# Block-sparse attention with routed experts and a feed-forward: scores over the used keys alone, masks and identity loaded once, another order of loads

## The chip, the cores and the metric

The kernel runs on one core of a Trainium2 chip. The metric is the device time of one launch in microseconds (us). The kernel before took 432.42 us as the median of three runs (431.78, 432.42 and 434.9).

## What is computed

Three layers follow one another. Shapes: batch 2, 8 heads, 576 positions, 64 columns per head; so 1,152 tokens of 512 columns.

```python
scores = q @ k.T / 8                              # per batch and head
mask_local   = (0 <= i - j) & (i - j < 32)        # heads 0 to 3
mask_strided = (0 <= i - j) & (i % 32 == j % 32)  # heads 4 to 7
attn = softmax(where(mask, scores, -1e9)) @ v     # heads side by side: x [1152, 512]
e = argmax(x @ w_gate);  gate = max(softmax(x @ w_gate))   # one of 8 experts
y = gate * (relu(x @ w1[e]) @ w2[e])              # w1 [8, 512, 1024], w2 [8, 1024, 512]
h = y @ w_in;  out = (h - tanh(h)) @ w_out        # w_in [512, 2048], w_out [2048, 512]
```

## The kernel before

Attention comes first, then routing, the experts and the feed-forward. The change touches attention alone, and the loads that are issued during it.

**Tiles.** Two heads of a batch are worked on together as a *pair*; there are eight, in the order of line 282: two local ones, four strided ones, two local ones. A local pair has nine tiles: 128 rows (64 positions of two heads) against the 96 keys that they can see. A strided pair has eleven tiles: positions are sorted by their remainder modulo 32, and a tile has 108 rows (three remainders times 18 positions of two heads) against the 54 keys of the same remainders. Tiles are worked on in *groups* of three (local) or four, four and three (strided): 24 groups, numbered 0 to 23, three per pair, so groups 3, 6, 9, 12 and 15 are the first of pairs 1 to 5.

**A group's steps.** `attn_scores` writes the mask of the whole group into a PSUM bank with one bfloat16 matmul by the identity, and then adds each tile's scores with one float32 matmul, which the trace shows as two instructions. The mask and the scores are as wide as a tile has rows: 128 or 108 columns, though only 96 or 54 are read afterwards. VectorE and ScalarE do the softmax. Three groups later `attn_probs_t` transposes the probabilities on TensorE with the float32 identity `identf`; five groups later `attn_values` multiplies them with the values. Seven groups after a pair's last group (`logits_pair`, n - LAG2 - 2) the rows of x are transposed back, multiplied with the gate's weights (both in one matmul against `iw`, which holds identity and gate side by side) and stored to DRAM by SP. The loop at line 523 issues these steps in this order, and each engine's instructions keep it.

**Loads.** All but one are issued by SP in program order; an issue that waits holds up those behind it. Queries and keys have two buffers, values three (`vts`), so a pair's load waits for the scores of the pair before the last. `load_qk` for pair i + 1 is called at the first group of pair i, its values (`load_v`) at the last. The first pair comes in pieces, and between them the masks, of which the loads bring all six local tiles and the strided ones; behind them pair 0's values, the identity in four copies (256 KB) and the gate. SP hands at most eight transfers to the queue before the oldest has landed. The two halves of the first expert's first weights (`load_w`, 1,024 KB each) are issued at groups 6 and 9, at group 9 behind the stores of pair 0's rows of x; from group 10 on their conversion to two float16 parts runs in between on ScalarE and VectorE.

**POOL** clears the unused rows of value and probability buffers at the start and has nothing to do in attention after that.

**Names and lines.** The masks and the identity: lines 111 to 114. Clearing on POOL: lines 243 to 251. `load_qk`: 253 to 271. First loads: 283 to 287. `attn_scores`: 289 to 319. The loop and the calls of `load_w`: 523 to 564. In the trace the instructions of all engines but SP have line 75, that of a helper, so they are told apart by their tiles: `kt,qt` the scores, `mk` the masks, `iw,pr` the transposes, `ptl,vt` and `ptr,vt` the values, `iw,xT` the logits, `st` a half of expert weights, `xd<-xw` the stores of x.

Of the kernel before, what the change touches and what calls it, by code (L numbers as in the profile page):

```python
# [8 lines left out]
BF16 = mybir.dt.bfloat16  # L9
# [12 lines left out]
E, F1 = 8, 1024  # L22
# [36 lines left out]
# h - tanh(h) by odd powers of h from the third on  # L59
# [5 lines left out]
class _Last:  # L65
    """An engine that remembers its last instruction."""
# [15 lines left out]
def kernel(  # L82
# [12 lines left out]
    @contextmanager  # L95
    def behind():
        # what the block adds on ACT and DVE is issued after what they have so far
        with tc.issue_after(act.last.ins), tc.issue_after(dve.last.ins):
            yield
# [11 lines left out]
    iw = cst.tile([P, NCH, P + E], F32, name="iw")  # L111
    identf = iw[:, 0, 0:P]
    mk = cst.tile([P, 3 * P + 3 * P + 4 * SM + P], BF16, name="mk")
    identb, ml0, mlb, msb = mk[:, 0:P], mk[:, P:4 * P], mk[:, 4 * P:7 * P], mk[:, 7 * P:]
# [14 lines left out]
    # sums of the low parts: not finite where a high part is not  # L129
# [4 lines left out]
    # sums of squares of a part of each operand, over their least  # L134
# [25 lines left out]
    def f64_split(hi, lo, raw, scale, n=512):  # L160
        # the bits of -w 2^128 as a float32; sizes from 1 on come out as not finite. A shift by three leaves the two
        # top bits of the exponent set; the last three bits of the fraction are the top ones of the low word
# [34 lines left out]
    def get_w(w, e, n=2):  # L197
        # the halves, and what splits them bit by bit
# [24 lines left out]
    KT = STRIDE + S + 64  # L223
    vts = [pa1.tile([P, NST * P], F32, name=f"vt{i}") for i in range(3)]
# [5 lines left out]
    # the clock of the products' array rises while the first rows are on their way  # L230
# [11 lines left out]
    # rows past the keys stay zero: the products take all 128 rows  # L242
# [6 lines left out]
    pool.memset(vts[2], 0.0)  # L249
    for t in ptr:  # L250
        pool.memset(t, 0.0)

    def load_qk(b, hp, first=False):
        qt = pa.tile([P, NST * P], F32, tag="q", name="qt")
        kt = pa.tile([P, KT], F32, tag="k", name="kt")
        if first:
            # what the first group of tiles takes goes first
            sp.dma_start(mk[:, :4 * P], masks[:, :4 * P])
            sp.dma_start(qt[:, : 3 * P], q_loc[b, hp, :, :3 * P])
            nc.scalar.dma_start(kt[:, :2 * P], k_loc[b, hp, :, :2 * P])  # L260
            sp.dma_start(mk[:, 4 * P:], masks[:, 4 * P:])
            sp.dma_start(kt[:, 2 * P:], k_loc[b, hp, :, 2 * P:])
            for j in (3, 6):
                sp.dma_start(qt[:, j * P:(j + 3) * P], q_loc[b, hp, :, j * P:(j + 3) * P])
        elif hp < 2:
            sp.dma_start(qt[:, : NLT * P], q_loc[b, hp])
            sp.dma_start(kt, k_loc[b, hp])
        else:
            sp.dma_start(qt[:, : NST * SM], q_str[b, hp - 2])
            sp.dma_start(kt[:, : NST * SN], k_str[b, hp - 2])  # L270
        return qt, kt
# [9 lines left out]
    # the last ones are local: only their last tiles' tokens wait for the end  # L281
    pairs = [(0, 0), (0, 1), (0, 2), (0, 3), (1, 2), (1, 3), (1, 0), (1, 1)]
    qks = {0: load_qk(*pairs[0], first=True)}
    vs_ = {}
    vs_[0] = load_v(0, *pairs[0])
    sp.dma_start(iw[:, :, 0:P], ident_d)
    sp.dma_start(iw[:, :, P:P + E], w_gate)

    def attn_scores(b, hp, tiles, qt, kt):
# [3 lines left out]
        w = nq  # L293
        sc = bank()
        mask = msb if not loc else (ml0 if tiles[0] == 0 else mlb)
        pe.matmul(sc[:, : n * w], identb, mask[:, : n * w], start=True, stop=False, skip_group_check=True)
        for j, i in enumerate(tiles):
            k0 = 64 * i if loc else SN * i
            wk = min(w, NST * SN - k0) if not loc else w
# [757 lines left out]
```

## Time and profile before

| | |
|---|---|
| median of three runs | 432.42 us (431.78 to 434.9) |
| profiled execution, its span from the first to the last instruction | 432.6 us (no other time of this execution is given) |
| TensorE (PE) matmuls busy | 399.6 us, 92% |
| VectorE (DVE) busy | 298.4 us, 69% |
| ScalarE (ACT) busy | 261.6 us, 60% |
| GpSimd (POOL) busy | 39.3 us, 9% |
| moved by DMA | 69.92 MB, mean 162 GB/s |
| granted TensorE clock, mean | 0.969 of 2.4 GHz |

Attention is about the first 82 us, routing and the first gather reach to 104 us, the experts to 240 us, the feed-forward to the end. Busy shares over the whole span say little here, because attention, a fifth of the span, has other limits than the rest. The page's row of granted clock shows three dips, in the slices around 15, 45 to 50, and 100 us. Sizes in the views of transfers are in units of 1,024 bytes; GB/s are of 10^9 bytes. A matmul's own duration includes its way through the array, so the spacing of a stream is read from the start of one to the start of the next.

### The profile page before, as it was taken

Reading aid. Unit: us, or ns where it says so; the run is one execution under the profiler, and the core shown is the slowest. Engines: PE = TensorE matmul, PEld = TensorE weight load, DVE = VectorE, ACT = ScalarE, POOL = GpSimd, SP = SyncE. Lnnn points to the kernel's source line nnn. Section 1 sums busy time; section 2 is a strip of 40 time slices with the busy share of each in tenths; the row PEclk is TensorE's granted clock in tenths of the full one; section 3 lists DMA queues with packets and bytes.
Section 4 is the critical chain, followed back from the end, with each engine's and each line's share of the span. In section 5 each row is a group of like instructions: output and inputs, shape, how many; then the busy total and the mean of one; then the engine's idle time right before and its main releaser. Section 6 shows DMA issues by size and latency. Waiting matters only on the chain.

```text
span 432.6 us, 8410 instructions
## 1 busy us (share of the span) xinstructions
PE 399.6 (92%) x3192; PEld 298.5 (69%) x3192; DVE 298.4 (69%) x752; ACT 261.6 (60%) x612; POOL 39.3 (9%) x44
## 2 busy tenths in 40 slices
PE   6699598864999999999999999999999999999994
PEld 3598598723999999999999566665444655444441
DVE  2388589772898979899999799999983678000000
ACT  3377387443996777876974799899752887100000
POOL 6000000066102011000000000000000100000000
PEclk9699699995999999999999999999999999999998
DMA  8797488626879788789724423312350100000000
GB/s 217 218 295 230 152 269 236 213 93 205 291 262 354 279 291 302 243 302 341 259 101 148 147 97 113 131 59 89 99 194 17 58 1 2 24 27 27 24 26 27
DMA packets 33514, 69.92 MB, mean 162 GB/s; under 512 B 3108, under 2 KB 9252, under 8 KB 33468
## 3 DMA queue, kind: packets, MB, share of 16 engines
q1 hardware_dynamic: 31580, 63.68, 44.7%
q0 software_dynamic: 1744, 5.51, 3.8%
q8 instruction: 27, 0.44, 0.4%
q14 instruction: 19, 0.16, 0.1%
q10 hardware_dynamic: 144, 0.13, 0.1%
HBM read 64.59 MB, written 4.72 MB: 160 GB/s over the span
## 4 chain that ended last, share of the span: by engine, by line
PE 42%; DVE 9%; issue 8%; DMA 3%; ACT 2%; POOL 0%; POOLq 0%; DVEq 0%; ACTq 0%
PE bank L75 42%; DVE w2l L75 3%; DMA xg<-xd,ids 2%; DVE w1l L75 2%; DVE fa L75 2%; DVE hl L75 1%; ACT w2h L75 1%; DMA out_dram<-ob,ids 1%; ACT win_h L75 1%; DVE x2l L75 0%; DVE xl L75 0%; DVE win_l L75 0%; ACT x2h L75 0%; POOL xg L75 0%; POOL out_dram L75 0%
## 5 line engine op out<-in xcount | busy, mean ns | idle before, releaser
L75 PE MATMUL bank<-xh,w1h 128*128 128x192 f16 x256 | 64.0, 250 | 7.6 <-ACT xh L75 7.6
L75 PE MATMUL bank<-xh,w1l 128*128 128x192 f16 x256 | 64.1, 250 | 0.7 <-DVE w1l L75 0.5
L75 PE MATMUL bank<-xl,w1h 128*128 128x192 f16 x256 | 64.0, 250 | 0.0
L75 PE MATMUL bank<-x2l,win_h 128*128 128x384 f16 x192 | 62.6, 326 | 0.5 <-DVE ok L75 0.5
L75 PE MATMUL bank<-hl,w2h 128*128 128x192 f16 x256 | 63.0, 246 | 0.0
L75 PE MATMUL bank<-hh,w2h 128*128 128x192 f16 x256 | 63.0, 246 | 0.0
L75 PE MATMUL bank<-hh,w2l 128*128 128x192 f16 x256 | 63.0, 246 | 0.0
L75 PE MATMUL bank<-x2h,win_h 128*128 128x384 f16 x192 | 62.6, 326 | 0.0
L75 PE MATMUL bank<-x2h,win_l 128*128 128x384 f16 x192 | 62.6, 326 | 0.0
L75 PEld LDWEIGHTS <-win_h 128*128 128x128 f16 x384 | 37.6, 98 | 25.8 <-DVE ok L75 0.7
L75 PE MATMUL bank<-wo_h,gh 128*128 128x512 f16 x144 | 54.6, 379 | 0.0
L75 PE MATMUL bank<-wo_l,gh 128*128 128x512 f16 x144 | 54.6, 379 | 0.0
L75 PE MATMUL bank<-wo_h,gl 128*128 128x512 f16 x144 | 54.6, 379 | 0.0
L75 PEld LDWEIGHTS <-gh 128*128 128x128 f16 x288 | 28.1, 98 | 33.6
L75 PEld LDWEIGHTS <-w1h 128*128 128x128 f16 x512 | 47.2, 100 | 0.3
L75 PEld LDWEIGHTS <-w2h 128*128 128x128 f16 x512 | 46.1, 98 | 0.0
L75 DVE SCALAR_TENSOR_TENSOR fa<-raw,fa 128x512 uint32<-128x512 uint32 x64 | 42.8, 684 | 2.1 <-ACT fa L75 1.7
L75 ACT ACTIVATE ob<-bank 128x512 f32<-128x512 f32 x9 | 5.4, 597 | 62.6 <-PE bank L75 60.1
L75 DVE SCALAR_TENSOR_TENSOR w2l<-st,w2h 128x1024 f16<-128x1024 f32 x32 | 38.8, 1217 | 2.9 <-ACT w2h L75 2.6
L75 DVE SCALAR_TENSOR_TENSOR w1l<-st,w1h 128x1024 f16<-128x1024 f32 (+1 forms) x40 | 38.4, 1003 | 0.3 <-ACT w1h L75 0.2
L75 DVE SCALAR_TENSOR_TENSOR w<-z,y 128x384 f32<-128x384 f32 x48 | 26.0, 552 | 15.2 <-ACT z L75 15.2
L75 PE MATMUL bank<-kt,qt 128*108 128x108 f32 (+2 forms) x160 | 23.5, 292 | 12.1 <-DMA kt<-in_k_str_dram 5.7
(144 smaller groups left out, 765.5 us busy)
## 6 DMA issues: line engine op xcount, KB each, us to landing
st<-in_w_dram SPq DMA_DIRECT2D x32, 1024.0 KB, 5.8
raw<-in_w_in_dram SPq DMA_DIRECT2D x16, 512.0 KB, 5.6
raw<-in_w_out_dram SPq DMA_DIRECT2D x16, 512.0 KB, 3.5
qt<-in_q_str_dram SPq DMA_DIRECT2D x4, 594.0 KB, 6.0
xd<-xw SPq DMA_DIRECT2D x15, 128.0 KB, 2.0
vt<-in_v_loc_dram SPq DMA_DIRECT2D x4, 432.0 KB, 6.1
qt<-in_q_loc_dram SPq DMA_DIRECT2D x3, 576.0 KB, 9.0
kt<-in_k_str_dram SPq DMA_DIRECT2D x4, 297.0 KB, 6.7
```

The costliest lines, as they stand in the source:

```text
L75: self.last = f(*a, **k)
```

## The change

- **Scores.** The score matmuls take the 96 or 54 keys that are read, and the bank is as narrow. The group's mask is read from one tile of the mask, repeated by the access pattern; only the first local group of a pair has its own mask columns.
- **Masks and identity.** Of the masks the first 128 KB are loaded as before, and of the strided one a single tile of 54 columns. The four float32 copies of the identity are no longer loaded, but written by POOL from the bfloat16 one; the gate is loaded to a tile of its own and copied by POOL to its place beside them.
- **Keys.** Keys have two fixed buffers whose margins POOL clears once; loads bring 576 columns and no margins (672 and 594 before).
- **Order on SP.** The first pair's pieces come without masks in between. Pair 1's queries and keys are issued right behind, in front of pair 0's values; its queries come in two pieces with the keys between them. The strided mask, the values and the gate follow.
- **Order on POOL.** The margins first; the three copies after the clearing of `vts[0]`, `vts[1]` and `ptl`; the clearing of `vts[2]` and `ptr` behind the copies.
- **Weights.** The two halves are issued at groups 5 and 8 instead of 6 and 9, that is behind the values of pairs 2 and 3 and in front of the queries and keys of pairs 3 and 4; the second half is now in front of the stores of pair 0's rows of x.

```diff
-    mk = cst.tile([P, 3 * P + 3 * P + 4 * SM + P], BF16, name="mk")
-    identb, ml0, mlb, msb = mk[:, 0:P], mk[:, P:4 * P], mk[:, 4 * P:7 * P], mk[:, 7 * P:]
+    mk = cst.tile([P, 4 * P + SN], BF16, name="mk")
+    identb, ml0, ml1, ms1 = mk[:, 0:P], mk[:, P:4 * P], mk[:, 2 * P:2 * P + KW], mk[:, 4 * P:]
...
+    kts = [pa1.tile([P, KT], F32, name=f"kt{i}") for i in range(2)]
...
+    for t in kts:
+        pool.memset(t[:, :STRIDE], 0.0)
+        pool.memset(t[:, STRIDE + S:], 0.0)
...
-    pool.memset(vts[2], 0.0)
-    for t in ptr:
-        pool.memset(t, 0.0)
-    def load_qk(b, hp, first=False):
+    def load_qk(n, b, hp):
         qt = pa.tile([P, NST * P], F32, tag="q", name="qt")
-        kt = pa.tile([P, KT], F32, tag="k", name="kt")
-        if first:
+        kt = kts[n % 2]
+        def keys(eng, c0, c1):
+            eng.dma_start(kt[:, STRIDE + c0:STRIDE + c1],
+                          k_loc[b, hp, :, STRIDE + c0:STRIDE + c1] if hp < 2 else k_str[b, hp - 2, :, c0:c1])
+        def queries(c0, c1):
+            sp.dma_start(qt[:, c0:c1], (q_loc[b, hp] if hp < 2 else q_str[b, hp - 2])[:, c0:c1])
+        if n == 0:
             sp.dma_start(mk[:, :4 * P], masks[:, :4 * P])
-            sp.dma_start(qt[:, : 3 * P], q_loc[b, hp, :, :3 * P])
-            nc.scalar.dma_start(kt[:, :2 * P], k_loc[b, hp, :, :2 * P])
-            sp.dma_start(mk[:, 4 * P:], masks[:, 4 * P:])
-            sp.dma_start(kt[:, 2 * P:], k_loc[b, hp, :, 2 * P:])
-            for j in (3, 6):
-                sp.dma_start(qt[:, j * P:(j + 3) * P], q_loc[b, hp, :, j * P:(j + 3) * P])
-        elif hp < 2:
-            sp.dma_start(qt[:, : NLT * P], q_loc[b, hp])
-            sp.dma_start(kt, k_loc[b, hp])
+            queries(0, 3 * P)
+            keys(nc.scalar, 0, 2 * P)
+            queries(3 * P, 6 * P)
+            keys(sp, 2 * P, S)
+            queries(6 * P, 9 * P)
+        elif n == 1:
+            queries(0, 3 * P)
+            keys(sp, 0, S)
+            queries(3 * P, 9 * P)
         else:
-            sp.dma_start(qt[:, : NST * SM], q_str[b, hp - 2])
-            sp.dma_start(kt[:, : NST * SN], k_str[b, hp - 2])
+            queries(0, NLT * P if hp < 2 else NST * SM)
+            keys(sp, 0, S)
         return qt, kt
...
-    qks = {0: load_qk(*pairs[0], first=True)}
+    qks = {i: load_qk(i, *pairs[i]) for i in range(2)}
+    wg = cst.tile([P, NCH, E], F32, name="wg")
+    sp.dma_start(mk[:, 4 * P:], masks[:, 7 * P:7 * P + SN])
     vs_ = {}
     vs_[0] = load_v(0, *pairs[0])
-    sp.dma_start(iw[:, :, 0:P], ident_d)
-    sp.dma_start(iw[:, :, P:P + E], w_gate)
+    sp.dma_start(wg, w_gate)
+    pool.tensor_copy(identf, identb)
+    pool.tensor_copy(iw[:, 1:, 0:P], identb.unsqueeze(1).to_broadcast([P, NCH - 1, P]))
+    pool.tensor_copy(iw[:, :, P:], wg)
+    pool.memset(vts[2], 0.0)
+    for t in ptr:
+        pool.memset(t, 0.0)
...
         nq, nk = (P, KW) if loc else (SM, SN)
-        w = nq
         sc = bank()
-        mask = msb if not loc else (ml0 if tiles[0] == 0 else mlb)
-        pe.matmul(sc[:, : n * w], identb, mask[:, : n * w], start=True, stop=False, skip_group_check=True)
+        scv = sc[:, : n * nk].rearrange("p (t k) -> p t k", k=nk)
+        if loc and tiles[0] == 0:
+            mask = ml0.rearrange("p (t k) -> p t k", k=P)[:, :, :nk]
+        else:
+            mask = (ml1 if loc else ms1).unsqueeze(1).to_broadcast([P, n, nk])
+        pe.matmul(scv, identb, mask, start=True, stop=False, skip_group_check=True)
         for j, i in enumerate(tiles):
-            k0 = 64 * i if loc else SN * i
-            wk = min(w, NST * SN - k0) if not loc else w
-            pe.matmul(sc[:nq, j * w:j * w + wk], qt[:, i * nq:(i + 1) * nq], kt[:, k0:k0 + wk],
+            k0 = 64 * i if loc else STRIDE + SN * i
+            pe.matmul(sc[:nq, j * nk:(j + 1) * nk], qt[:, i * nq:(i + 1) * nq], kt[:, k0:k0 + nk],
                       start=False, stop=True, skip_group_check=True)
...
-            if g == 0 and i + 1 < len(pairs):
-                qks[i + 1] = load_qk(*pairs[i + 1])
+            if g == 0 and 1 < i + 1 < len(pairs):
+                qks[i + 1] = load_qk(i + 1, *pairs[i + 1])
...
-        if n in (6, 9):
-            w10.append(load_w(1, n // 9, 0))
+        if n in (5, 8):
+            w10.append(load_w(1, n // 8, 0))
```

## Rows read from the trace of the kernel before

**Rows 1.** Busy time by stretch: engines, granted clock, DMA share, GB/s.

```profile
60.00:80.00 20.00, 18.03 (x157) 16.77 (x156) 18.23 (x85) 14.40 (x63) 0.00 (x0) 1.00 0.89 294
110.00:240.00 130.00, 128.99 (x1561) 127.85 (x1558) 118.85 (x221) 98.61 (x155) 8.80 (x10) 1.00 0.76 261
```

**Rows 2.** Waits of TensorE to 60 us: us in total, times, longest.

```profile
PE bank L75 <- DMA kt<-in_k_str_dram: 5.7, 1, 5.7
PE bank L75 <- DMA kt<-in_k_loc_dram: 5.5, 1, 5.5
PE bank L75 <- DVE zz L75: 1.2, 1, 1.2
```

**Rows 3.** Timeline of TensorE: start, us, instructions, idle before and releaser.

```profile
15.11 1.62 PE L75 MATMUL bank<-kt,qt 128*128 128x128 f32 x6 [5.49 <-DMA kt<-in_k_loc_dram]
...
21.77 0.35 PE L75 MATMUL bank<-mk 128*128 128x432 bf16 x1
...
27.30 0.35 PE L75 MATMUL bank<-mk 128*128 128x432 bf16 x1
27.48 0.92 PE L75 MATMUL bank<-kt,qt 128*108 128x108 f32 x8
...
34.54 0.35 PE L75 MATMUL bank<-mk 128*128 128x432 bf16 x1
...
38.16 0.36 PE L75 MATMUL bank<-mk 128*128 128x432 bf16 x1
...
41.99 0.35 PE L75 MATMUL bank<-mk 128*128 128x432 bf16 x1
47.99 1.75 PE L75 MATMUL bank<-kt,qt 128*108 128x108 f32 x8 [5.66 <-DMA kt<-in_k_str_dram]
...
53.03 0.36 PE L75 MATMUL bank<-mk 128*128 128x432 bf16 x1
```

**Rows 4.** Busy time by stretch, around the second wait.

```profile
42.00:44.00 2.00, 0.34 (x3) 0.00 (x0) 1.45 (x7) 2.00 (x10) 0.00 (x0) 1.00 1.01 320
44.00:46.00 2.00, 0.00 (x0) 0.00 (x0) 1.94 (x7) 1.29 (x5) 0.00 (x0) 0.60 0.98 322
46.00:48.00 2.00, 0.01 (x1) 0.04 (x1) 1.31 (x6) 0.00 (x0) 0.00 (x0) 0.50 0.84 227
50.00:52.00 2.00, 2.00 (x15) 1.99 (x14) 0.33 (x2) 1.45 (x6) 0.00 (x0) 0.69 0.07 29
```

**Rows 5.** Timeline of SP: when transfers are issued.

```profile
0.74 0.39 SPq L258 DMA_DIRECT2D mk<-in_masks_dram  x1
...
21.36 0.41 SPq L270 DMA_DIRECT2D kt<-in_k_str_dram  x1
...
26.89 0.41 SPq L270 DMA_DIRECT2D kt<-in_k_str_dram  x1
32.99 0.39 SPq L391 DMA_DIRECT2D xd<-xw  x1
...
34.66 0.46 SPq L184 DMA_DIRECT2D st<-in_w_dram  x1
...
36.14 0.56 SPq L270 DMA_DIRECT2D kt<-in_k_str_dram  x1
```

**Rows 6.** The same issues (0.74, 21.36, 26.89, 34.66): KB, us to landing.

```profile
mk<-in_masks_dram SPq DMA_DIRECT2D x1, 128.0 KB, 2.7
kt<-in_k_str_dram SPq DMA_DIRECT2D x1, 297.0 KB, 4.2
kt<-in_k_str_dram SPq DMA_DIRECT2D x1, 297.0 KB, 6.7
st<-in_w_dram SPq DMA_DIRECT2D x1, 1024.0 KB, 7.9
```

**Rows 7.** Groups of instructions: busy us, mean ns | idle before; 83 to 85 us.

```profile
L75 PE MATMUL bank<-iw,xT 128*128 128x8 f32 x4 | 0.6, 262 | 0.0
```

**Rows 8.** Timeline of POOL.

```profile
5.33 1.28 POOL L75 MEMSET vt<- 128x1408 f32 x1
```

More of the change, by code (lines that the diff above doesn't have):

```diff
@@ L292, in attn_scores @@
         nq, nk = (P, KW) if loc else (SM, SN)
-        w = nq
         sc = bank()
-        mask = msb if not loc else (ml0 if tiles[0] == 0 else mlb)
-        pe.matmul(sc[:, : n * w], identb, mask[:, : n * w], start=True, stop=False, skip_group_check=True)
+        scv = sc[:, : n * nk].rearrange("p (t k) -> p t k", k=nk)
[4 more added lines that the diff above has]
+        pe.matmul(scv, identb, mask, start=True, stop=False, skip_group_check=True)
         for j, i in enumerate(tiles):
-            k0 = 64 * i if loc else SN * i
-            wk = min(w, NST * SN - k0) if not loc else w
-            pe.matmul(sc[:nq, j * w:j * w + wk], qt[:, i * nq:(i + 1) * nq], kt[:, k0:k0 + wk],
+            k0 = 64 * i if loc else STRIDE + SN * i
+            pe.matmul(sc[:nq, j * nk:(j + 1) * nk], qt[:, i * nq:(i + 1) * nq], kt[:, k0:k0 + nk],
                       start=False, stop=True, skip_group_check=True)
-        scv = sc[:nq, : n * w].rearrange("p (t k) -> p t k", k=w)[:, :, :nk]
+        scv = scv[:nq]
         mx = pa.tile([P, 4], F32, tag="mx", name="mx", bufs=4)
```

## The prediction

> **What bounds the kernel now.** I read the table of stretches first. From 110 to 240 us TensorE is busy 128.99 of 130 us at the full clock [rows 1], so whatever brings the end of attention forward arrives at the end of the kernel nearly undiminished, and a gain must be looked for before that. The waits of TensorE up to 60 us are almost all two waits for keys, 5.5 and 5.7 us [rows 2]. The timeline of TensorE dates them: pair 1's keys let group 3 begin at 15.11, pair 5's let group 15 begin at 47.99, though its mask product stood ready at 41.99 [rows 3]. While TensorE waits, its granted clock falls: 1.00 in 42 to 44 us, 0.60, then 0.50 (the level of 1.2 GHz, down from 2.4), and in 50 to 52 it is still 0.69 [rows 4]. So a wait is paid twice. The keys are late because of what SP issues ahead of them: in front of pair 5's keys (36.14) stand three stores of x that could only be issued from 32.99 on, and the 1,024 KB half of the first expert's weights (34.66) [rows 5].
>
> How fast does the queue deliver? The first mask slice lands at 0.74 + 2.7 = 3.44 us [rows 5, 6]. Pair 1's keys land at 15.11; by the tiles' shapes 2,732 KB stand between the two, which makes 234 KB per us. Later, from pair 3's keys (21.36 + 4.2 = 25.6) to pair 4's (26.89 + 6.7 = 33.6), weights, values, queries and keys are 1,024 + 297 + 594 + 297 = 2,212 KB in 8.0 us: 276 KB per us. The second weight half took 7.9 us from issue to landing, 130 KB per us [rows 5, 6], but it started behind the stores on a queue that had run dry. I take 234 up to pair 2 and the mean, 255, after it; 130 and 276 are kept as ends.
>
> **The change, part by part.**
>
> *Fewer and reordered bytes at the start.* Ahead of pair 1's keys go away: 204 KB of masks, 432 KB of pair 0's values, 256 KB of identity, 16 KB of gate, 384 KB of pair 1's later queries and 96 KB of margins, 1,388 KB. What is left is 1,344 KB, so these keys land at 3.44 + 1344/234 = 9.2 us, not 15.11. Pair 0's values now come behind 2,174 KB, at 12.7. Their first use is at the end of group 5; groups 3 to 5 took 21.77 - 15.11 = 6.7 us at half clock [rows 3], so no less than 3.3 now, 12.5 or later. A few tenths may be lost, and the next wait hides them.
>
> *Where the wait goes.* Pair 2's keys have 3,504 KB in front and land at 18.4. TensorE asks for them between 12.5 and 15.9 (9.2 + 6.7), so it waits 2.5 to 6 us at group 6. That group began at 21.77 [rows 3]: 3.4 us are won so far, not 5.9.
>
> *Weights in front.* Each half now goes ahead of a pair's queries and keys. Small tables (121 KB) end at 18.9. Then values 297, weights 1,024, queries 594, keys 288, that is 2,203 KB: pair 3's keys at 18.9 + 8.6 = 27.5, where group 9 began at 27.30 [rows 3]; TensorE gets there at 18.4 + 5.1 = 23.5 (27.30 - 21.77, less 0.4 for narrower products; at half clock 18.4 + 6.7 = 25.1, which this wait hides). The same bundle again, with the second half in it: pair 4's keys at 36.1, against 34.54 before, TensorE ready at 27.5 + 6.8 = 34.3. Then the stores (288 KB), values, queries, keys, 1,467 KB: pair 5's keys at 41.9. Group 15's turn is 36.1 + 7.1 = 43.2 (41.99 - 34.54, less 0.35), so there is no wait. The second weight half no longer stands behind the stores on SP, and the stores, late anyway, go behind it. Its splits follow from group 16 on and wait for nothing.
>
> So group 15's scores begin at 43.3 in place of 47.99, and without the low clock the way to the next mask is that of group 12, 38.16 - 34.54 = 3.6, less 0.1, not 53.03 - 47.99 = 5.0 [rows 3]. Group 16 stands at 46.8: 6.2 us earlier.
>
> *Narrower scores.* For the mask product the columns are the cost: 432 take 27.48 - 27.30 = 0.18 us, so half of them saves 0.09 per strided group, a quarter of 384 saves 0.04 per local one [rows 3]. For the scores the rows say otherwise. Eight float32 matmuls of 108 moving columns under 108 stationary ones run in 0.92 us, 95 ns apart, and four with only 8 moving columns, but 128 stationary, in 0.6 us at 262 ns each, (0.6 - 0.26)/3 = 113 ns apart [rows 3, 7]. The load of the stationary side sets the pace, and that is not narrowed; I grant only the last matmul of a group, 0.045 and 0.027 us. From group 16 on this is 2 x 0.13 + 6 x 0.067 = 0.6 us; before that it shortens steps that then wait for keys.
>
> The Trainium skill, page TensorE: Matmul & The Clock Gate, section Back-to-back issue gap, has the spacing of an isolated stream go with the moving columns. By it each score matmul would get cheaper by a half (strided) or a quarter (local), which is rival D below; the row with 8 columns speaks against it, and the same page's section on LDWEIGHTS, where the time goes with the stationary columns, agrees with that row.
>
> *Identity on POOL.* Three copies of 128, 384 and 32 columns are not in the trace. A memset of 1,408 columns takes 1.28 us [rows 8]; at that rate they are 0.5 us, at four times that 2.0. The memsets that stay in front of them end at 5.33 now, a few tenths later with the margins', and the first transpose stands behind group 3's scores, after 9.2 us: hidden. The gate's copy waits for the gate's landing (2,190 KB, 12.8 us), and behind it on POOL stands the clearing of the third value buffer, 1.3 us; the load of pair 2's values, and SP's queue behind it with the weights, is released at 14.2. The queue has work until 18.9, so this is hidden with 4 us to spare. Keys in two fixed buffers wait as the rotating ones did; the four margin memsets run in the first 2 us.
>
> *VectorE.* From 60 to 80 us it is busy 18.23 of 20 us [rows 1], and in the second wait it worked off 1.45 + 1.94 + 1.31 = 4.7 us [rows 4]. That respite is gone. I charge 1 us (between 0 and 4.7), near the low end, since before 60 us TensorE never waits for it for longer than 1.2 us [rows 2].
>
> **Sum.** 6.2 + 0.6 - 1 = 5.8 us off. The profiled span is 432.6 us, 0.2 above the median of the three runs, 432.42; so 426.7 us is forecast. With 276 KB per us throughout the later part pair 4's keys come at 34.9 and the gain is 7; with 234 they come at 37.7 and it is 4.2: 425.4 to 428.3.
>
> **Rivals.**
> A, slower: the weights hold the keys up. If each half takes 7.9 us, as the second one did, and the rest goes at 234, a bundle takes 13.0 us: pair 3's keys at 31.9, pair 4's at 44.9, group 16 at 55.5, 2.5 late, with up to 3 more for the clock after a wait of several us: 435 to 438. It decides from about 6.7 us per half. For it: the one landing that the profile shows. Against: the other half lay inside the 8.0 us bundle.
> B, larger gain: the queue delivers what the DMA moved in 42 to 46 us, 320 GB/s [rows 4], 312 KB per us. Then pair 2's keys land at 14.7, pair 3's at 22.2, group 16 comes near 40, 13 us early, and VectorE gives some back: 421. Against: such rates are means over all DMA engines, and a tile is there when the slowest is done.
> C, given back: VectorE needs the 4.7 us that the wait gave it, and the end of attention moves by 2 only: 430.2.
> D, the pace of the score matmuls goes with the moving columns after all: groups 15 to 23 hold 22 strided ones, 0.045 us each, and 36 local ones, 0.027 each, 2.0 us more: 424.7. That is what the first of the two sections of the Trainium skill's page named above would give.
>
> **How the numbers follow.** Forecast 0.52, A 0.13, B 0.13, C 0.17, D 0.05. About 1%, 4.3 us, is what a measurement here can tell from no change. Faster by more than that: B, D and five sixths of the forecast, 0.62. Slower: half of A, 0.06. The rest, 0.32, is within. The range goes from B's 421 to 431.5, past C; it leaves out A and a part of B.
>
> **What would show it.** Right: the first wait for keys gone from 10 to 15 us; waits at groups 6 and 9, ending near 18.4 and 27.5; none at group 15; score matmuls still 95 and about 112 ns apart; group 16's mask near 46.8; the stretch after attention as long as before. Wrong: weight halves landing over 6.7 us after the transfer ahead of them; TensorE waiting for VectorE before group 20; a first transpose that waits for POOL.

## The result and the profile after

The changed kernel takes 428.7 us (median of 20 runs, 424.4 to 432.9), the kernel before in the same session 432.8 (20 runs): ratio 0.9897, 95% interval 0.987 to 0.9924. That is 4.1 us faster, where 5.8 us and 426.7 were forecast: inside the range, 2.0 us above the forecast and 1.5 below rival C (430.2). The steps came out rather differently than forecast.

Profiled span: 426.8 us, of an execution that took 428.67. The table gives the start of the named matmul (or of VectorE's write of the slots' ids) in each trace, in us.

| kernel | median us | ratio to before [95%] | group 16 | last logits | ids | first expert matmul | first of feed-forward | span |
|---|---|---|---|---|---|---|---|---|
| before | 432.78 | | 53.03 | 83.36 | 88.23 | 103.66 | 239.36 | 432.64 |
| after | 428.70 | 0.9897 [0.987, 0.9924] | 42.71 | 75.84 | 80.71 | 96.86 | 233.51 | 426.80 |
| e1_weights_late | 428.47 | 0.9952 [0.992, 0.9984] | 47.60 | 78.18 | 83.05 | 98.07 | 232.66 | 425.93 |
| e2_values_first | 427.79 | 0.9912 [0.9874, 0.9951] | 44.29 | 75.82 | 80.69 | 96.30 | 233.02 | 426.31 |
| e3_wide_scores | 426.53 | 0.9887 [0.9844, 0.993] | 44.77 | 76.66 | 81.53 | 96.81 | 232.11 | 425.38 |
| e5_no_low_parts | 421.03 | 0.9767 [0.9732, 0.9802] | 47.81 | 77.08 | 81.95 | 92.33 | 227.23 | 420.51 |
| e8_bytes_alone | 428.62 | 0.9902 [0.9866, 0.9938] | 50.41 | 80.13 | 85.02 | 100.66 | 236.90 | 430.18 |
| g1_bytes_back | 432.07 | 0.9988 [0.995, 1.0026] | 46.81 | 79.95 | 84.83 | 100.42 | 236.52 | 429.96 |
| e4_early_splits | 421.23 | 0.9727 [0.9686, 0.9769] | 44.37 | 74.74 | 79.61 | 90.36 | 225.99 | 419.64 |
| e7_first_tokens_first | 428.22 | 0.9903 [0.9868, 0.9937] | 42.14 | 75.22 | 80.09 | 87.79 | 231.38 | 424.87 |
| e9_gather_alone | 430.39 | 0.9957 [0.9927, 0.9987] | 42.55 | 75.93 | 80.81 | 88.62 | 232.94 | 426.21 |
| f2_low_parts_later | 422.03 | 0.9758 [0.9721, 0.9796] | 45.05 | 76.63 | 81.51 | 89.98 | 227.94 | 421.23 |
| f3_weights_behind_rows | 425.71 | 0.9852 [0.9815, 0.9889] | 42.81 | 75.74 | 80.62 | 91.96 | 228.89 | 422.18 |
| f4_early_and_later | 420.89 | 0.9757 [0.9709, 0.9806] | 43.58 | 73.98 | 78.85 | 89.34 | 223.39 | 416.68 |

Sessions ran beside different medians of before (432.78; 431.03 for e1, e2, e3, e5; 432.37 for e4, e7, e8, e9; 432.87 for f2 to f4; 432.22 for g1), so kernels are compared by their ratios. One row of a trace is one execution, and those of a kernel differ by up to 8.5 us. Up to the last logits after, e7, e9, f2 and f3 are the same program, and in these five traces group 16 lies at 42.1 to 45.1 and the last logits at 75.2 to 76.6: smaller differences than that between two rows say little. Ratios leave out executions over 1.5% above the fastest of their kernel; one of those left out, of f3, took 1,045 us, which nothing here explains.

The waits of TensorE to 60 us, which answer to [rows 2] (total, times, longest):

```profile
PE bank L75 <- DMA kt<-in_k_str_dram: 3.4, 2, 2.5
PE bank L75 <- DVE nm L75: 2.1, 1, 2.1
PE bank L75 <- DVE zz L75: 1.2, 1, 1.2
```

The two long waits for keys, 11.2 us, have become two short ones of 3.4, and a new one for VectorE has come. The timeline of TensorE, for [rows 3]:

```profile
8.27 0.88 PE L75 MATMUL bank<-kt,qt 128*128 128x96 f32 x6
...
11.23 0.50 PE L75 MATMUL bank<-iw,pr 128*96 128x128 f32 x3 [2.08 <-DVE nm L75]
...
14.42 0.26 PE L75 MATMUL bank<-mk 128*128 128x216 bf16 x1
15.56 0.93 PE L75 MATMUL bank<-kt,qt 128*108 128x54 f32 x8 [0.88 <-DMA kt<-in_k_str_dram]
...
20.75 0.26 PE L75 MATMUL bank<-mk 128*128 128x216 bf16 x1
23.54 1.01 PE L75 MATMUL bank<-kt,qt 128*108 128x54 f32 x8 [2.54 <-DMA kt<-in_k_str_dram]
...
28.41 0.27 PE L75 MATMUL bank<-mk 128*128 128x216 bf16 x1
28.52 0.88 PE L75 MATMUL bank<-kt,qt 128*108 128x54 f32 x8
...
32.08 0.26 PE L75 MATMUL bank<-mk 128*128 128x216 bf16 x1
...
39.22 0.26 PE L75 MATMUL bank<-mk 128*128 128x216 bf16 x1
...
42.71 0.27 PE L75 MATMUL bank<-mk 128*128 128x216 bf16 x1
```

Group 3's scores start at 8.27 without a wait (15.11 before), group 6's at 15.56, group 9's at 23.54; groups 12 and 15 wait for nothing, and group 16 stands at 42.71, 10.3 us earlier. When SP issues, for [rows 5], and the last two issues' time to landing, for [rows 6]:

```profile
8.71 0.43 SPq L261 DMA_DIRECT2D kt<-in_k_str_dram  x1
...
12.16 0.39 SPq L185 DMA_DIRECT2D st<-in_w_dram  x1
...
14.62 0.33 SPq L261 DMA_DIRECT2D kt<-in_k_str_dram  x1
...
19.67 0.38 SPq L185 DMA_DIRECT2D st<-in_w_dram  x1
...
20.64 1.11 SPq L261 DMA_DIRECT2D kt<-in_k_str_dram  x1
...
31.50 0.42 SPq L261 DMA_DIRECT2D kt<-in_k_str_dram  x1
```

```profile
kt<-in_k_str_dram SPq DMA_DIRECT2D x1, 288.0 KB, 10.2
kt<-in_k_str_dram SPq DMA_DIRECT2D x1, 288.0 KB, 5.6
```

Pair 4's keys are there at 20.64 + 10.2 = 30.8 and pair 5's at 31.50 + 5.6 = 37.1, each before its group's turn. The stretches, for [rows 1] and [rows 4] (busy us of PE, PEld, DVE, ACT, POOL; granted clock; DMA share; GB/s):

```profile
42.00:44.00 2.00, 2.00 (x20) 1.68 (x19) 1.91 (x10) 0.35 (x1) 0.00 (x0) 1.00 0.91 338
44.00:46.00 2.00, 2.00 (x22) 2.00 (x22) 1.97 (x10) 1.61 (x9) 0.00 (x0) 1.00 0.05 15
60.00:80.00 20.00, 17.25 (x118) 13.71 (x118) 15.16 (x77) 10.53 (x39) 0.00 (x0) 0.91 0.70 218
100.00:230.00 130.00, 128.68 (x1544) 127.60 (x1542) 115.44 (x216) 97.75 (x153) 8.99 (x10) 0.99 0.77 264
```

Where before TensorE stood still for most of 42 to 46 us, it is busy throughout, at the full clock. From 100 to 230 us it is bound by itself as before.

### The profile page after: what moved, and what is told of

It is laid out like the page before. It is cut to its first block, busy times and chain, and to the rows that moved or that the text cites. A ratio compares the mean times of both kernels' runs of the same rounds, so it can differ in the third digit from the quotient of the medians.

```text
span 426.8 us, 8424 instructions
## 1 busy us (share of the span) xinstructions
PE 398.3 (93%) x3192; PEld 296.9 (70%) x3192; DVE 299.1 (70%) x752; ACT 261.0 (61%) x612; POOL 40.6 (10%) x51
## 4 chain that ended last, share of the span: by engine, by line
PE 61%; DVE 17%; issue 9%; DMA 9%; ACT 3%; POOL 0%; POOLq 0%; DVEq 0%; ACTq 0%
PE bank L75 61%; DMA xg<-xd,ids 4%; DVE w1l L75 3%; DVE w2l L75 3%; DMA kt<-in_k_str_dram 2%; DVE fa L75 2%; DMA qt<-in_q_str_dram 1%; DVE xT L75 1%; DVE hl L75 1%; DVE pr L75 1%; ACT w2h L75 1%; DVE mx L75 1%; DMA out_dram<-ob,ids 1%; ACT win_h L75 1%; DVE rs L75 1%
## 5 line engine op out<-in xcount | busy, mean ns | idle before, releaser
L75 ACT ACTIVATE w2h<-st 128x1024 f16<-128x1024 f32 (+1 forms) x33 | 34.3, 1045 | 0.0
```

The costliest lines, as they stand in the source:

```text
L75: self.last = f(*a, **k)
```

## The experiments

The time has three places: the start (to group 16), the rest of attention (to the last logits), and the way from the ids to the first expert matmul. On that way GpSimd issues *gathers*: transfers that fetch from DRAM the rows of x of an expert's tokens, by the ids, the first two for expert 0, the third and fourth for expert 1. ScalarE scales the rows by their gates, TensorE transposes them, and ScalarE and VectorE write them as two float16 parts, the *columns* that the experts' products take. Expert weights are split the same way: ScalarE writes the *high part*, VectorE the *low part*, in one instruction of about 0.7 us, here called a *split*. The first five kernels take the change apart; the others follow what happened to its gain.

**Weights late again.**
```
-        if n in (5, 8):
-            w10.append(load_w(1, n // 8, 0))
+        if n in (6, 9):
+            w10.append(load_w(1, n // 9, 0))
```


> The changed kernel with the two weight halves issued at groups 6 and 9 again. If bytes and order at the start made the gain and the weights' place is neutral, pair 3's keys no longer wait behind a half (no wait at group 9, 2.5 us in the changed kernel), group 15 waits up to 2 us, group 16 stands at 41 to 43 us (42.71 in the changed kernel) and the time is 428 to 430 us. If the weights' place is what removed the wait at group 15, that wait is back with 4 us or more, group 16 stands at 47 or later, and the time is 431 or more.


The wait for pair 5's keys at group 15 is back, though shorter than the 4 us that were named, and a stretch of low clock with it (1.2 GHz from 39.4 to 46.2 us): the earlier weights are what removed this wait.

```profile
42.25 1.66 PE L75 MATMUL bank<-kt,qt 128*108 128x54 f32 x8 [3.18 <-DMA kt<-in_k_str_dram]
```

Group 16 is 4.9 us later than in the changed kernel, and the last logits only 2.3 us. The ratio is 0.55% above that of the change, and the two intervals overlap by a hair: the earlier weights bring something like 2 us, not shown with certainty.

**Values first.**
```
-    qks = {i: load_qk(i, *pairs[i]) for i in range(2)}
+    qks = {0: load_qk(0, *pairs[0])}
...
     sp.dma_start(wg, w_gate)
+    qks[1] = load_qk(1, *pairs[1])
```


> The changed kernel with pair 1's queries and keys behind the strided mask, pair 0's values and the gate, as the order was before; everything else as changed. If the order of the first loads matters, group 3 waits some 2 us for keys (462 KB more in front, at 234 to 290 KB per us) and group 16 comes 1.5 to 2 us later, time 430 to 431. If softmax sets the start anyway (group 3's transposes waited for VectorE until 11.23), the later keys cost nothing: group 16 within 0.7 us of 42.71 and time 428 to 429.5.


No difference in time (0.9912 against 0.9897). In its trace group 3 does wait for its keys, 2.2 us, and group 16 comes 1.6 us later. The last logits come when those of the changed kernel do (75.82 against 75.84), but only because its last groups of attention ran at the full clock and the changed kernel's did not (below). Pair 1's keys ahead of pair 0's values are worth nothing that can be seen in the time.

**Wide scores.**
```
-        scv = sc[:, : n * nk].rearrange("p (t k) -> p t k", k=nk)
+        w = nq
+        scv = sc[:, : n * w].rearrange("p (t k) -> p t k", k=w)[:, :, :nk]
...
-            pe.matmul(sc[:nq, j * nk:(j + 1) * nk], qt[:, i * nq:(i + 1) * nq], kt[:, k0:k0 + nk],
+            wk = min(w, KT - k0)
+            pe.matmul(sc[:nq, j * w:j * w + wk], qt[:, i * nq:(i + 1) * nq], kt[:, k0:k0 + wk],
```


> The changed kernel with score matmuls 128 and 108 columns wide again (masks stay narrow; the columns past the keys are written and not read). If the load of the stationary side sets their pace, a group gets at most 0.045 us longer, spacing stays 95 and 112 ns, group 16 within 0.5 us of 42.71, time 428.5 to 429.3. If the moving columns set it in the changed kernel, the changed kernel's spacing is 51 and 84 ns and the wide one's groups are 0.36 (strided) and 0.16 (local) us longer, group 16 and the end 1.5 to 2.5 us later.


Ratio 0.9887 against 0.9897: the narrower scores bring nothing measurable. Group 16 was expected within 0.5 us of 42.71 and stands at 44.77; pair 2's keys came at 18.14 there instead of 15.56, with the same bytes in front of them, so the transfers are what differed. Its trace has a strided group of eight score matmuls in 0.92 us, the changed kernel's in 0.88:

```profile
44.88 0.92 PE L75 MATMUL bank<-kt,qt 128*108 128x108 f32 x8
```

**The bytes alone** (the smaller masks, the identity made on GpSimd, the gate's tile, the fixed key buffers; everything else as before): the three edits above together, with pair 1's queries loaded whole.
```
-    qks = {i: load_qk(i, *pairs[i]) for i in range(2)}
+    qks = {0: load_qk(0, *pairs[0])}
...
+    qks[1] = load_qk(1, *pairs[1])
...
-            queries(0, 3 * P)
-            keys(sp, 0, S)
-            queries(3 * P, 9 * P)
+            queries(0, 9 * P)
+            keys(sp, 0, S)
```


> Only one part of the change is kept: the masks' smaller copies, the identity made on GpSimd from the masks' tile, the gate's own tile and the fixed key buffers; the score matmuls are as wide as before, pair 1's queries and keys go behind pair 0's values and the gate, and the weight halves are issued at groups 6 and 9 as before. Theory Q (the queue delivers about 290 KB per us once it is full, and the fewer bytes are most of the gain): pair 1's keys, behind 2,300 KB instead of 2,732, land near 12 to 13 instead of 15.1, pair 2's near 16 to 18, the last wait for keys, at group 15, stays since weights and stores still stand in front of pair 5's keys, and the time is 1 to 2 us below the kernel before. Rival R (the order is what counts): the time is within 0.5 us of the kernel before. Rival V (any order does, since VectorE's work sets the end): the last logits start at 76 to 78 and the time is within 1.5 us of the changed kernel.


Ratio 0.9902, as fast as the changed kernel: 4.2 us of gain, 2.7 to 5.8 by the interval, where theory Q said 1 to 2. The places came as Q had them: pair 1's keys are there at 12.95 (15.11 before), and both long waits for keys remain, 4.6 us at group 3 and 4.9 at group 15. So, as far as one trace goes, removing these waits is not what the time hung on. It is the trace of the longest of this kernel's eight executions, 432.03 us, and its milestones are late for that reason among others. Weights late, which has the fewer bytes too and its weights in the same place, came out at 0.9952; the two intervals overlap, and the runs don't divide the gain more finely than that.

```profile
PE bank L75 <- DMA kt<-in_k_loc_dram: 5.0, 2, 4.6
```

```profile
44.54 1.75 PE L75 MATMUL bank<-kt,qt 128*108 128x108 f32 x8 [4.88 <-DMA kt<-in_k_str_dram]
```

**The bytes back** (orders and narrow scores stay, tables are loaded as before).
```
-            queries(3 * P, 6 * P)
+            sp.dma_start(mk[:, 4 * P:], masks[:, 4 * P:])
+            queries(3 * P, 6 * P)
...
-    sp.dma_start(wg, w_gate)
-    pool.tensor_copy(identf, identb)
...
+    sp.dma_start(iw[:, :, 0:P], ident_d)
+    sp.dma_start(iw[:, :, P:], w_gate)
```


> The changed kernel with its tables loaded as before: all 1,328 columns of the masks ahead of the second part of pair 0's keys, identity and gate by the queue behind pair 0's values, no copies on GpSimd. The orders of keys, values and weights and the narrow scores stay. About 209 KB more stand in front of pair 1's keys and 450 KB in front of pair 2's, 0.7 and 1.6 us at the 290 KB per us seen in the changed kernel. Theory Q (the fewer bytes are the gain, the orders add nothing, as the kernel with the bytes alone was as fast as the changed one): the gain is lost, 431.5 to 432.5 us beside about 432.5 for the kernel before. Rival S (either part is enough, since behind group 16 VectorE's work and then the gathers of rows set the pace and take back whatever comes earlier): the last logits start at 76 to 77.5 and the time stays at 428 to 429.5, ratio 0.988 to 0.993.


Ratio 0.9988: the gain is gone, as theory Q had it, and rival S is out. Group 15 waits no longer, group 16 stands at 46.81, and yet nothing is won by the end. TensorE now waits for the identity in front of its first transposes, since in the new order it stands behind pair 1's keys:

```profile
PE bank L75 <- DMA iw<-in_ident_dram: 4.3, 1, 4.3
```

So the fewer bytes are enough for the gain, and the orders without them bring none in this arrangement; one with the identity in front of pair 1's keys was not run.

**No low parts** (VectorE's low parts of expert 0's first weights are left out, GpSimd fills zeros in their place).
```
-                split_w(w10[i // 4], i % 4, 1)
+                st, hi, lo, sc = w10[i // 4]
+                act.activation(hi[:, i % 4, :], st[:, i % 4, :], AF.Copy, scale=sc)
+                pool.memset(lo[:, i % 4, :], 0.0)
```


> The changed kernel without the low parts of the first expert's first weights: VectorE's eight instructions (0.69 and 0.08 us each, 6.1 us in all, between groups 10 and 20) are left out, POOL writes zeros there, so the output is not the reference's. If VectorE is what gives back the gain of 10 us at group 16 (7.5 left at the last logits), TensorE does not wait for it at groups 21 to 26, the last logits come at 72 to 74 us instead of 75.84, and the time is 424.5 to 427. If something else gives it back, the last logits stay within 0.7 us of 75.84 and the time within 1 us of 428.7.


Ratio 0.9767, 1.3% (5.6 us) below that of the changed kernel, but not where it was looked for: the last logits are no earlier. The fills ran from 8.71 to 12.49, right behind the clearing that began at 6.30, and a tiny instruction of VectorE was held until their end, 5.88 us for what takes 0.17 elsewhere:

```profile
8.71 3.78 POOL L75 MEMSET w1l<- 128x512 f16 x8
```

```profile
6.63 5.88 DVE L75 TENSOR_SCALAR nm<-mx 128x3 f32<-128x3 f32 x1
```

From group 16 to the last logits it is the shortest of all, 29.3 us. Most of its gain came between ids and first expert matmul: 10.4 us instead of 16.1. This opened the second question.

**Early splits.**
```
-    W1_AT = [10, 11, 13, 14, 16, 17, 19, 20]
+    W1_AT = [8, 8, 9, 9, 10, 11, 12, 14]
...
-            if n in W1_AT:
-                i = W1_AT.index(n)
+            for i in [i for i, at in enumerate(W1_AT) if at == n]:
```


> The first weights of expert 0 are split at groups 8 to 14 instead of 10 to 20, into the time up to 32 us in which VectorE was busy 7 to 8 of 10 us; nothing else changes. Theory V (between groups 16 and 26 the work of VectorE, 9.3 to 9.6 of 10 us, sets when the last logits can start; that is where 2.5 of the changed kernel's 10.3 us went): about four splits of 0.69 + 0.08 us leave that stretch, the last logits start at 73 to 74 instead of 75.8 and the time is 2 to 3 us below that of the changed kernel, 424 to 426. Rival T (the chain of each group, scores to values, sets the pace by TensorE itself and its low clock at 68.6 to 72 us): the last logits stay at 75 to 76 and the time within 1 us. Rival W (the splits wait for the second weight half, landed at 28.7, and hold ScalarE and VectorE up): group 12 or 15 comes 1 to 3 us later and the time is 1 to 2 us longer.


421.2 us, ratio 0.9727, the fastest by the ratio and below both kernels. Theory and third rival both hold in part: group 16 is 1.7 us later (no more than one program's traces differ by), the way from there to the last logits 2.8 us shorter (30.4; about 1.5 of that is the low clock, see below), 1.1 us net. The larger part, 5.4 us, lies again behind the ids, where its third gather of rows was not held up.

**First tokens first.**
```
-            act.activation(xg, xg, AF.Copy, scale=gsl[:, a:a + 1])
+            with tc.issue_after(xh_done[0]) if e == 1 else nullcontext():
+                act.activation(xg, xg, AF.Copy, scale=gsl[:, a:a + 1])
...
+        xh_done.append(act.last.ins)
```


> One dependency is added to the changed kernel: on ScalarE the scaling of expert 1's first gathered rows goes behind expert 0's second half of token columns. Theory O (what was won by the end of attention is partly lost again because ScalarE stands 8.04 us in front of that scaling, whose gather of rows lands at 95.69, while expert 0's columns are ready to be made at 87.7): the first expert matmul starts at 88.5 to 90 instead of 96.86, and since the next expert then waits for the same rows, at 97 to 98, some of it is lost again: the time is 3 to 7 us below the changed kernel's, 421 to 425. Rival P (weights or the low parts, not the columns, are the last to be ready): the first expert matmul stays after 95 and the time within 1 us.


The first expert matmul starts at 87.79, 9 us earlier, and the time does not move (0.9903). The wait has only moved: expert 1's transposes stand on TensorE behind the first quarter of expert 0's products, and there it waits 5.9 us for the same rows. A wait was removed, its cause was not.

**Gather alone** (the edit above, and the six splits of expert 1's weights placed behind the first four gathers).


> The kernel with the one dependency on ScalarE, and also the six splits of expert 1's first weight halves put behind the first four gathers of rows. Theory G (GpSimd's third issue of an indirect transfer takes 4.38 us instead of 0.92 because VectorE splits weights at the same time, 84.23 to 88.4 us, and its rows then land behind the weights that the first gather releases): that issue takes about 0.9 to 1.4 us, the rows land near 88 to 90 instead of 95.69, expert 1 finds its columns ready, and the time is 2 to 5 us below that of the kernel with the dependency alone. Rival N (the issue is slow for another reason): it still takes about 4 us and the rows land after 94, the time within 1 us of that kernel, or longer by up to 3 us as the splits come later.


The issue took 0.92 us as expected, the time did not follow (0.9957): ScalarE now had the eight high parts, and pieces of expert 0's second weights, in front of expert 1's rows, and TensorE met the same wait:

```profile
96.88 1.54 PE L75 MATMUL bank<-iw,xg 96*128 96x96 f32 x8 [5.60 <-ACT xg L75]
```

**Low parts later** (only VectorE's six low parts go behind the gathers; ScalarE's high parts stay).
```
-            split_w(w11[i // 4], i % 4, 1)
+            split_hi(w11[i // 4], i % 4)
...
+    with behind():
+        for i in range(NB):
+            split_lo(w11[i // 4], i % 4)
     w1s[1], w2s[0] = [ld[1:3] for ld in w11], [ld[1:3] for ld in w20]
```


> The changed kernel with VectorE's six low parts of expert 1's first weights moved behind the first four gathers of rows; ScalarE's high parts stay where they were. Theory G (VectorE's run of splits holds up the gather that GpSimd issues within a microsecond of its start: in the traces so far that issue ended 0.79 us after the last split, and the weights that the splits release then travel in front of the rows): the third issue takes about 0.9 us instead of 4.4, its rows land near 88 instead of 95.7, the first expert matmul starts at 89 to 91 instead of 96.9, and the time is 4 to 6 us below the changed kernel's, 422 to 425. Attention is untouched, the last logits stay at 75 to 76.5. Rival X (the weights ahead of the rows on the queues alone, not the issue): the issue is short but the rows still land after 93. Rival Y (the low parts, later now, are missed by expert 1): the gain in front of expert 0 is lost again before expert 1 and the time is within 1.5 us.


Theory G's numbers came true: issue 0.92 us, rows at 88.3, first expert matmul at 89.98, 422.0 us (only the last logits, 76.63, are a little later than it said). First the changed kernel's third gather and VectorE's first and last split, then this kernel's (the transfer rows give us to landing):

```profile
84.38 4.38 POOL L75 DMA_INDIRECT xg<-xd,ids  x1 [0.30 <-DVE gsl L75]
```

```profile
84.23 0.68 DVE L75 SCALAR_TENSOR_TENSOR w1l<-st,w1h 128x512 f16<-128x512 f32 x1
...
87.29 0.68 DVE L75 SCALAR_TENSOR_TENSOR w1l<-st,w1h 128x512 f16<-128x512 f32 x1
```

```profile
xg<-xd,ids POOLq DMA_INDIRECT x1, 11.3
```

```profile
85.19 0.92 POOL L75 DMA_INDIRECT xg<-xd,ids  x1 [0.30 <-DVE gsl L75]
```

```profile
xg<-xd,ids POOLq DMA_INDIRECT x1, 3.1
```

In the changed kernel the issue ended at 88.76, 0.79 us after the last split. Its rows came 11.3 us after the issue began, 3.1 without the splits.

**Weights behind rows.**
```
     rows = gather(0)
-    first_gather.append(pool.last.ins)
...
     rows = gather(1)
+    first_gather.append(pool.last.ins)
```


> The changed kernel, with the loads that wait for the first expert's rows made to wait for the second expert's rows as well; the order of every engine stays. Theory G says that both the slow third issue and the weights in front of its rows make them late: with the weights held back the rows land at about 89 + 2.5 = 91.5 instead of 95.7, the first expert matmul starts near 92.7 instead of 96.9, and the time is 2 to 4 us below the changed kernel's, if the held weights (landing some 5 us later) are not missed. Rival I (the slow issue alone, its descriptors being late): the rows still land after 94 and the time is within 1 us or up to 2 us longer.


The issue is as slow as in the changed kernel (4.38 us), the rows land at 90.8 instead of 95.7 and the first expert matmul starts at 91.96: of the 7.4 us that the rows came late (95.7 against 88.3 with the low parts later), about 5 were the weights in front of them. The ratio, 0.9852, is 0.45% below that of the change; the intervals overlap.

**Early and later** (early splits, low parts later, and first tokens first).


> Three edits together on the changed kernel: expert 0's first weights are split at groups 8 to 14, the low parts of expert 1's first weights come behind the first four gathers, and ScalarE scales expert 1's rows behind expert 0's columns. If the early splits bring 1 to 1.5 us by the end of attention and the rest of their 7 us came from gathers that were no longer held up, the first expert matmul starts at 87.5 to 89 (90.4 with the early splits alone) and the time is 417 to 420.5, at or below the 421.2 of the early splits alone. Rival Z (the start of the experts is then bound by the second expert's rows or weights): the first expert matmul is early, but expert 0's second products stay at 109 to 110 and the time is 420.5 to 422.


420.9 us, ratio 0.9757: faster than both kernels, not shown to be faster than the early splits alone. The time is in rival Z's range, but expert 0's second products did not stay at 109 to 110: they begin at 107.1, so neither account is settled. Its profiled span, 416.7, is the shortest of all, of the fastest of its six executions.

## Why the prediction was right, and where it was not

**The delivery rate was mis-sized.** I took 234 and then 255 KB per us. In front of pair 2's keys stood 3,504 KB; they came between 3.44 and 15.56, 289 KB per us. The bundle with the second weight half, 2,203 KB, took from 23.54 to 30.8, 303 KB per us. This is rival B's mechanism at nearly its figure (312). In the five traces of this program pair 2's keys came between 15.56 and 16.25, 274 to 289 KB per us. The 234 was no measure of the queue: between 3.44 and 15.11 the DMA moved 271 GB/s in before, 265 KB per us, so more than the bytes that I had counted in front of pair 1's keys. With the higher rate the keys came at 15.6, 23.5, 30.8 and 37.1 where I had 18.4, 27.5, 36.1 and 41.9. The term of 6.2 us at group 16 became 10.3. The waits stand where they were forecast, at groups 6 and 9 and none at 12 and 15, only shorter. Rival A is out: a bundle took 7.3 us, not 13.

**VectorE was sized about right, the clock was not foreseen.** From group 16 to the last logits the changed kernel needs 33.1 us, before 30.3. The stretch in five kernels, before, after, low parts later (the same program up to here), values first and early splits:

```profile
53.00:83.40 30.40, 28.18 (x242) 26.04 (x241) 26.96 (x121) 20.46 (x83) 0.00 (x0) 1.00 0.75 240
```

```profile
42.70:75.80 33.10, 30.21 (x241) 27.25 (x240) 28.50 (x128) 21.10 (x87) 0.00 (x0) 0.95 0.73 234
...
64.00:68.00 4.00, 2.85 (x26) 2.34 (x24) 3.83 (x28) 2.64 (x12) 0.00 (x0) 1.00 1.06 381
68.00:72.00 4.00, 3.30 (x18) 3.30 (x19) 2.62 (x11) 1.06 (x3) 0.00 (x0) 0.58 0.62 206
```

```profile
45.00:76.60 31.60, 28.91 (x242) 25.69 (x240) 28.58 (x128) 21.16 (x87) 0.00 (x0) 1.00 0.73 230
...
68.00:72.00 4.00, 2.62 (x24) 2.42 (x24) 3.86 (x27) 1.66 (x6) 0.00 (x0) 1.00 0.94 335
72.00:76.00 4.00, 4.00 (x34) 3.38 (x32) 2.95 (x12) 1.06 (x4) 0.00 (x0) 1.00 0.64 161
```

```profile
44.30:75.80 31.50, 28.71 (x241) 25.66 (x240) 28.45 (x128) 21.18 (x87) 0.00 (x0) 1.00 0.71 230
```

```profile
44.40:74.70 30.30, 27.70 (x241) 25.41 (x240) 27.13 (x124) 20.25 (x84) 0.00 (x0) 1.00 0.77 238
```

With the same 128 instructions of VectorE the stretch takes 33.1 us where the granted clock falls, to a mean of 0.58 in 68 to 72 us, and 31.6 where it stays at 1.00: about 1.5 us for the level of 1.2 GHz. The other traces agree: with the low clock in this stretch first tokens first, gather alone, weights behind rows and the bytes back take 32.9 to 33.4 us, and values first, without it, 31.5. What made it fall is not shown: TensorE was busy 2.85 of the 4 us before, and 2.62 of 4 in the other kernel, where it did not fall. The other 1.3 us, 31.6 against 30.3, are VectorE's: with the splits taken out of the stretch (27.1 us busy instead of 28.6) it takes 30.3 as before. The kernel before has as many splits behind group 16 as the changed one, four, but VectorE had caught up in the long wait. So the charge of 1 us was near, and rival C's mechanism real at a quarter of its 4.7 us. That a low clock would come back at another place was not in the text.

**"The stretch after attention as long as before" failed by 1.7 us.** From the last logits to the first expert matmul it went from 20.3 to 21.0 us, the experts from 135.7 to 136.7. The first is the third gather, whose rows landed 14.3 us after the ids before and 15.0 after; it was held up in both kernels. The second was not followed.

**The sum came out right by errors that cancel, which is luck.** Trace against trace: 10.3 - 2.8 - 0.7 - 1.0 = 5.8 us, my number (whose terms, 2 x 0.13 + 6 x 0.067 for the narrower scores, add up to 0.66 and not 0.6). The medians differ by 4.1 only. In all profiled executions whose own time is known, that time is 1.75 to 1.9 us above the span, so the profiled one of before took about 434.5, some 2 us above its median, and not 0.2 as I read it. The gain between traces, taken off the median, gave 426.7; taken off 434.5 it gives 428.7. (The 434.5 is worked out from the other traces; the time of that execution is not recorded.)

**Narrower scores: right.** Eight strided scores take 0.88 us in place of 0.92, the pace between them did not move (95 ns from the second on), and undoing them costs nothing measurable. Rival D is out. The Trainium skill, page TensorE: Matmul & The Clock Gate, section LDWEIGHTS (loading the stationary operand), has the time of that load go with the stationary columns, and the trace agrees: the 108 are unchanged, and so is the pace.

**The identity on GpSimd: hidden, but not what stands behind it.** The casts took 0.74 us, ending at 6.4. They push the clearing of value and probability buffers to 6.30 to 8.77, and there VectorE's second instruction of the first softmax, 0.17 us elsewhere, was held until the clearing ended:

```profile
6.30 1.28 POOL L75 MEMSET vt<- 128x1408 f32 x1
7.51 1.26 POOL L75 MEMSET ptr<- 128x432 f32 x3
```

```profile
6.81 1.97 DVE L75 TENSOR_SCALAR nm<-mx 128x3 f32<-128x3 f32 x1
...
8.84 0.17 DVE L75 TENSOR_SCALAR nm<-mx 128x3 f32<-128x3 f32 x1
```

That is the new wait of 2.1 us for VectorE, in front of group 4: TensorE waiting for VectorE before group 20 was one of the signs that I had named for being wrong. I had looked at who waits for GpSimd by a semaphore, not at who shares something with it. By the trace it cost nothing here: without it TensorE would have stood longer at group 6, whose keys came 0.9 us later than TensorE as it was. And the clearing ran in front of the gate's copy (12.04), not behind it as I had it: pair 2's values were issued at 11.78 and not held to 14.2.

**What my text did not separate** was the bytes from the orders. The 6.2 us stood on both; by the runs the bytes alone reach the changed kernel's time, and the orders without them, in the one arrangement that was run, bring nothing. Nor does it look like the two long waits: in the trace of the bytes alone both are still there. Why the bytes alone reach that time is settled only in part. With the weights late, the scores wide or the low parts left out, group 16 is 2.1 to 5.1 us later than in the changed kernel and the last logits only 0.8 to 2.3. About 1.5 us of what they make good is the low clock, which none of the three has in this stretch; the rest, with the weights late and without the low parts, goes with less work of VectorE there (26.1 and 25.3 us busy instead of 28.5). With the bytes back, whose stretch has the low clock too, 4.1 us at group 16 are 4.1 at the last logits. The trace of the bytes alone comes from that kernel's longest execution, so its own milestones don't decide it.

## What to carry to other kernels

Count the bytes ahead of the first use before reordering them, and give what an engine can make from data already there to an idle one. When a wait goes, look who used it to catch up: the next bound was VectorE, then a gather held up by VectorE's own work, and moving work of VectorE (eight splits earlier, or six low parts later) brought another 1.4 to 1.7% (6 to 7 us), more than the whole change. A wait that is taken away without its cause, as in front of expert 0's columns, turns up at the next instruction that needs the same rows. And set a forecast against the median only after asking how the profiled run stands to it.

## What the runs showed of the hardware

**GpSimd and VectorE hold each other up.** Fills on GpSimd held a VectorE instruction of 0.17 us for 0.47 us in before and 0.72 in the bytes back, in both to the end of the fill that was running, and for 1.97 in after and 5.88 in no low parts, to the end of a whole series of fills. In the other direction, in before, after, e1, e2, e3, e7, e8, f3 and g1 the third gather, begun 0.1 to 0.8 us after the first of six splits, took 3.8 to 4.4 us and ended 0.79 us after the last; with the splits elsewhere 0.92. The Trainium skill, page SBUF — State Buffer, section Who interferes with whom, says that the two share a pair of ports, that an instruction of VectorE in a two-port mode and one of GpSimd block each other fully, for the whole instruction (one with two inputs in SBUF, as the splits have, blocks only what reads SBUF on GpSimd), and that a transfer issued by GpSimd is held up when it can't get port time to make its descriptors. The rows agree that one holds up the other; but here it lasted over several instructions, six splits or four fills and more. And in one place they don't agree: with the early splits and without the low parts the third gather began in the middle of the same splits and took 0.92 us, and the second, begun 0.7 us after the first split, no more than 1.4. Early splits, GpSimd and then VectorE's first and last split:

```profile
83.80 1.39 POOL L75 DMA_INDIRECT xg<-xd,ids  x1 [0.30 <-issue]
85.49 0.92 POOL L75 DMA_INDIRECT xg<-xd,ids  x1 [0.30 <-issue]
```

```profile
83.10 0.68 DVE L75 SCALAR_TENSOR_TENSOR w1l<-st,w1h 128x512 f16<-128x512 f32 x1
...
86.15 0.68 DVE L75 SCALAR_TENSOR_TENSOR w1l<-st,w1h 128x512 f16<-128x512 f32 x1
```

What decides between the two stays open.

**The low clock comes back elsewhere.** Each trace has a few stretches at the level of 1.2 GHz, 3 to 17 us long. Before has them at 13.7 to 20.5, 44.4 to 51.2 and 99 to 109 us, after at 24 to 28, 68.6 to 72 and 92.5 to 103. Where they fall is not fixed by the program alone: of the five traces that are the same program up to the last logits, one has none between 8 us and group 16 (which then stands at 42.1), three have one of 3.4 us (42.6 to 42.8), and one has 6.8 us (45.1); from group 16 to the last logits four have one and one has none. So that taking a wait away moved them is not shown. In before, the part that fell behind the second wait made the way from group 15's scores to group 16's mask 5.0 us, where group 12 took 3.6 with its mask; inside the last groups of attention of the changed kernel such a stretch cost 1.5 us.
